# The first two attention tiles of a fused attention and two-layer MoE kernel: their heads in the hand-made order, a later start of the weight conversion, and two unread products per head

## Chip, cores and metric

The kernel runs on one core of one Trainium2 chip. The metric is the device time of one execution in microseconds. The kernel before takes 914.15 us (median of 3 runs, 914.04 to 915.16).

## What is computed

The reference is windowed causal attention over 4 batches, 8 heads, 576 positions and 64 columns a head (window 128, linear position bias), followed by a dense layer pair on all 2304 tokens and a mixture of 8 experts that sends each token to one expert. Cut to what matters:

```python
scores = where((rel >= 0) & (rel < 128), q @ k.T / 8 - slope[h] * abs(rel), -1e9)
x = softmax(scores) @ v                      # 2304 tokens x 512
x = (s * relu(x @ w_in)**2 + b) @ w_out      # 512 -> 2048 -> 512, dense
e = argmax(normalised(x) @ normalised(emb).T / tau)
out = gate * (relu(x @ w1[e]) @ w2[e])       # one of 8 experts per token
```

## The kernel before

**Tiles and heads.** The 2304 tokens are 18 tiles of 128. A tile has 8 heads, so there are 144 pairs of tile and head (called heads here, u = 8 t + h). Tiles 0 and 9 look at one tile of keys, the others at two. The first four tiles (`t < NRAW`) use the float32 inputs as they arrive (`raw`).

**One tick.** `tick` issues, in this order on TensorE (PE): the scores of head n (`stage_A`, L242), the value product of head n-4 (`stage_D`, L301), the transposes of head n-2 (`stage_C`, L278) and, once in four heads, the transposes of four finished heads (`stage_T`, L330). Around them stand, in the order of the string `'BX.C.M.G.N...'`: on VectorE (DVE) the bias and row minimum of head n (`stage_B`, L254) and the scaling of finished heads (`stage_X`); on ScalarE (ACT) the copy of the transposed head n-2 out of PSUM (`stage_C2`, L283, tile `PW`) and the exponential of head n (`stage_N`, L262). Each of the seven dots is a call of `pt`, which adds `rate[0]` to an account and takes one step of the conversion queue whenever the account reaches 1. The score banks are `bank[0:4]` in turn, so every fourth head uses `bank[3]`.

**The conversion.** The dense weights `w_in` and `w_out` come as 32 chunks of 512 KB into four `stage` buffers. A chunk is split in four steps of the queue: a load that refills a free buffer, a cast on ACT (L181), a merge on DVE (L185), and a last step with one instruction on ACT (L193) and one on DVE (L194). ACT and DVE work through their instructions in the order in which they were issued.

**The unread products.** `warm(n)` issues n products 128x128 by 128x512 of zeros in bfloat16 into `bank[3]` (L747); nothing reads them. Nine stand at the very start.

**The stretch of the change.** `ticks(2)` is 21: the 16 heads of tiles 0 and 1 and the first five of tile 2. The first 4 ticks stand inside `tc.manual_schedule()`, which leaves the order as written; the next 17 are ordered by the planner, by its own costs. Behind them a loop over `SK` = 8 weight chunks (called the first dense loop here) interleaves two heads with the first dense block's products `L1` (L351) and `L2` (L374); `first` and `second` force conversion steps where a chunk isn't there yet. That loop stays with the planner.

Of the kernel before, what the change touches and what calls it, by code (L numbers as in the profile page):

```python
# [43 lines left out]
def moe_attention_kernel(ctx, tc, qT, kT, vN, w_in, w_out, sc_s, sc_b, bneg, tri, bmix,  # L44
# [190 lines left out]
    def stage_A(u, S):  # L235
        t, h, order, sl, bc, n = geom(u)
        pr, odd = divmod(h, 2)
        hb = slice(64, 128) if odd else slice(0, 64)
        o = S[:, 0:n]
        if t < NRAW:  # L240
            for i, k in enumerate(order):
                nc.tensor.matmul(S[:, i * P:(i + 1) * P], lhsT=raws[1][t][hb, pr, :], rhs=raws[0][k][hb, pr, :], start=True, stop=True)  # L242
            return
        Q, K, L = (sp.QO, sp.KO, sp.LO) if odd else (sp.QE, sp.KE, sp.LE)
        nc.tensor.matmul(o, lhsT=Q[:, pr, :], rhs=K[:, pr, sl, :], start=True, stop=False)
        nc.tensor.matmul(o, lhsT=Q[:, pr, :], rhs=L[:, pr, sl, :], start=False, stop=True)

    def stage_B(u, S):
        t, h, order, sl, bc, n = geom(u)
        s, st = sbuf(u)[:, 0:n], st_r[u % 4]  # L250
        bi, c = (bias8[h], -0.125) if t < NRAW else (bias, 2.0 ** -(h + 1))
        if t in MIXED or t in AFTER_MIXED:
            bi, bc = bmx[t in AFTER_MIXED], slice(0, 256)
        nc.vector.tensor_tensor_reduce(s, S[:, 0:n], bi[:, bc], scale=c, scalar=3.0e38,  # L254
                                       op0=ALU.add, op1=ALU.min, accum_out=st[:, 0:1])
# [18 lines left out]
    def stage_C(u, PO):  # L274
        t, h, order, sl, bc, n = geom(u)
        p = sbuf(u) if t < NRAW else sp.p[u % 2]
        for i in range(len(order) if t < NRAW else 1):
            nc.tensor.transpose(PO[:, i * 128:(i + 1) * 128], p[:, i * 128:(i + 1) * 128], ident)  # L278

    def stage_C2(u, PO):  # L280
        t, h, order, sl, bc, n = geom(u)
        if t < NRAW:
            nc.scalar.activation(PW[u % 2][:, 0:n], PO[:, 0:n], AF.Copy)  # L283
            return
        pc, pp = (PP[u % 2][:, i] for i in range(2))
        nc.scalar.activation(pp if n > P else pc, PO[:, 0:P], AF.Copy)
        if n > P:
            nc.gpsimd.tensor_tensor(pc, pp, sp.tri, op=ALU.mult)
            nc.gpsimd.tensor_tensor(pp, pp, pc, op=ALU.subtract)
# [4 lines left out]
    def stage_D(u, PO):  # L294
        t, h, order, sl, bc, n = geom(u)
        last = len(order) - 1
        if t < NRAW:
            o = outs(u)[:, h % 4 * 64:(h % 4 + 1) * 64]
            for i, k in enumerate(order):
                v = raws[2][k].rearrange("p c f -> p (c f)")[:, h * 64:(h + 1) * 64]  # L300
                nc.tensor.matmul(o, lhsT=PW[u % 2][:, i * P:(i + 1) * P], rhs=v, start=i == 0, stop=i == last)  # L301
            return
        for i, k in enumerate(order):
            nc.tensor.matmul(PO[:, 0:P], lhsT=sp.V[k % 3][:, h // 2, :], rhs=PP[u % 2][:, t - k], start=i == 0, stop=i == last)

    def stage_X(u, PO, part=2):
        t, h = divmod(u, H)
        if t < NRAW:
            if h % 4 == 3 and part != 0:
                g = u // 4 % 2  # L310
                rs, xs = rs_r[g], xs_r[g]
                nc.vector.tensor_scalar(rs, su_r[t % 2][:, h - 3:h + 1], 1e-9, None, op0=ALU.add)
                nc.vector.reciprocal(rs, rs)
                nc.vector.tensor_tensor(xs.rearrange("p (h d) -> p h d", h=4), outs(u).rearrange("p (h d) -> p h d", h=4),
                                        rs.unsqueeze(2).to_broadcast([P, 4, 64]), op=ALU.mult)
            return
        pr, odd = divmod(h, 2)
        hb = slice(64, 128) if odd else slice(0, 64)
        blk, c = divmod(t, 2)
        xh, xl = (x[hb, pr, c * P:(c + 1) * P] for x in xbuf(blk))  # L320
        o = PO[hb, 0:P]
        if part != 1:
            nc.scalar.activation(xh, o, AF.Copy)
        if part != 0:
            nc.vector.tensor_tensor(xl, o, f32(xh), op=ALU.subtract)

    def stage_T(u):
        g = u // 4 % 2
        for i in range(2):
            nc.tensor.transpose(bank[4 + g][:, 256 + i * P:256 + (i + 1) * P], xs_r[g][:, i * P:(i + 1) * P], ident)  # L330
# [77 lines left out]
    def run(ops):  # L408
        for f in ops:
            if callable(f):  # L410
                f()
# [173 lines left out]
    rate, due = [0.0], [0.0]  # L585
# [9 lines left out]
    def plan_preps(t, h):  # L595

        if t < NRAW:
            return
        if h in (0, 1):
            preps.ops += prep_q(t, 2 + h)  # L600
            if h == 1 and t + 1 < NT:
                preps.ops.append(lambda: load_qkv(t + 1, 1))
        if t + 1 < NT:
            if h == HK:
                preps.ops += prep_k(t + 1)
                if t + 2 < NT:
                    preps.ops.append(lambda: load_qkv(t + 2, 0))
            if h == HV:
                preps.ops.append(lambda: load_qkv(t + 1, 2))
            if h in (5, 6):  # L610
                preps.ops += prep_q(t + 1, h - 5)
# [11 lines left out]
    def unit(n):  # L623

        n -= LAG if n >= NRAW * H + LAG else 0
        return n if 0 <= n < UN else None

    def ticks(t):

        return t * H + LAG + (LAG - 1 if t > NRAW else 0)  # L630

    OR0, OR, OR1 = 'BX.C.M.G.N...', '.BUC..VME.G[..R]', 'BUC.VE...MG[].R.'
    def tick(Sb, POb, mid=None, attend=True, Ob=None):
        n = nu[0] if attend else 2 * UN
        if attend:
            nu[0] += 1
        u, c, d, x = (None if NRAW * H <= i < NRAW * H + LAG else unit(i) for i in (n, n - 2, n - LAG + 1, n - LAG))
        if u is not None:
            S = Sb[u % len(Sb)]
            plan_preps(*divmod(u, H))  # L640
            stage_A(u, S)
        if d is not None:
            POd = Ob[d % len(Ob)] if Ob else POb[d % len(POb)][:, 256:512]
            stage_D(d, POd)
        if c is not None:
            POc = POb[c % len(POb)]
            stage_C(c, POc)
        turn = x is not None and x % 4 == 3 and x < NRAW * H
        if turn:
            stage_T(x)  # L650
        def B():
            if u is not None:
                stage_B(u, S)

        def X():
            if d is not None:
                stage_X(d, POd)

        def U():
            if d is not None:  # L660
                stage_X(d, POd, 0)

        def V():
            if d is not None:
                stage_X(d, POd, 1)

        def C():
            if c is not None:
                stage_C2(c, POc)

        def N():
            if u is not None:
                stage_N(u)
            if turn:
                stage_Y(x)

        def E():
            if u is not None:
                stage_N(u, 0)
            if turn:  # L680
                stage_Y(x)

        def R():
            if u is not None:
                stage_N(u, 1)

        def M():
            if mid is not None:
                mid(0)

        def G():
            if mid is not None:
                mid(fill if '[' in od else ())
            elif '[' in od:
                run(fill)

        fs = dict(E=E, R=R, U=U, V=V, B=B, X=X, C=C, N=N, M=M, G=G)
        od = OR0 if n < NRAW * H else (OR if mid is not None else OR1)
        fill = [pt if z == '.' else fs[z] for z in od[od.find('[') + 1:od.find(']')]] if '[' in od else []
        od = od[:od.find('[') + 1] + od[od.find(']') + 1:]  # L700
        for z in od:
            if z == '[':
                continue
            if z == '.':
                pt()
            else:
                fs[z]()
# [8 lines left out]
    wide = (bank[0:4], bank[4:8])  # L716
# [9 lines left out]
    HK, HV = 2, 5  # L726
    SK = 8
    J3 = 4
    LEAD = 4

    def need(c):
        while len(done) <= c:
# [11 lines left out]
    def warm(n):  # L744

        for _ in range(n):
            nc.tensor.matmul(bank[3], lhsT=zero[:, 0:P], rhs=zero, start=True, stop=True)  # L747

    warm(9)
    with tc.manual_schedule():  # L750
        for i in range(LEAD):
            tick(*wide)
            warm(1)
            if i == 1:
                rate[0] = 0.17
    for i in range(LEAD, ticks(2)):
        tick(*wide)
        warm(1)
    rate[0] = 0.4
    for j in range(SK):  # L760
        def mid(i):
# [339 lines left out]
```

## Time and profile before

| | |
|---|---|
| median of 3 runs | 914.15 us |
| the profiled execution | 915.15 us |
| its span | 913.4 us |
| PE busy | 896.0 us (98%) |
| ACT busy | 647.0 us (71%) |
| DVE busy | 642.2 us (70%) |
| mean granted clock of PE | 0.959 of 2.4 GHz |

The profile is of one execution. Busy times of PE are modelled from pipelined products: an engine that is busy all the time can still run at half its clock, so the granted clock is read beside them. The span leaves out some 1.75 us of the execution's own time.

### The profile page before, as it was taken

The page shows a single profiled execution, that of the slowest core. Times are in us where ns is not written, and L with a number is a line of the kernel's source. Part 1 is how long each engine was busy: PE and PEld are TensorE (multiplying, and loading weights), DVE is VectorE, ACT ScalarE, POOL GpSimd, SP SyncE. Part 2 cuts the span into 40 slices and gives each one's busy share as a digit, 9 for nine tenths or more (in the row PEclk, how much of TensorE's full clock was granted, in tenths as well). Part 3 has the DMA queues.
Part 4 walks back from the last instruction along what each step waited for, and adds up shares of the span by engine and source line. Part 5 has one row for each costly group of instructions (what it writes and reads, how often), then busy time and mean ns, then how long its engine had stood idle before and what let it go on. Part 6 is the DMA issues. An engine that isn't in the chain of part 4 may idle for free. (4 is left out here: it accounts for less than half of the span.)

```text
span 913.4 us, 17128 instructions
## 1 busy us (share of the span) xinstructions
PE 896.0 (98%) x5341; PEld 777.2 (85%) x5344; DVE 642.2 (70%) x1719; ACT 647.0 (71%) x1501; POOL 325.4 (36%) x553
## 2 busy tenths in 40 slices
PE   7999998999999999999999999999999999999997
PEld 4678877989999999999999999988888888888886
DVE  3336789656665676667666655467989999899895
ACT  4447897656676767666776753457889889888885
POOL 2000246554663266555655642111632111111101
PEclk7558999999999999999999999999999999999999
DMA  7224652010020102011200200456973795755300
GB/s 263 74 70 134 227 161 78 13 59 13 25 59 13 59 24 59 21 31 44 58 16 33 36 1 1 168 184 227 268 262 127 267 338 212 257 187 210 110 20 29
DMA packets 31600, 101.32 MB, mean 111 GB/s; under 512 B 8581, under 2 KB 9222, under 8 KB 24850
## 3 DMA queue, kind: packets, MB, share of 16 engines
q1 hardware_dynamic: 26562, 89.58, 29.4%
q0 software_dynamic: 4256, 9.46, 2.9%
q10 hardware_dynamic: 688, 1.15, 0.3%
q8 instruction: 43, 0.70, 0.3%
q14 instruction: 51, 0.42, 0.2%
HBM read 133.82 MB, written 10.92 MB: 158 GB/s over the span
## 5 line engine op out<-in xcount | busy, mean ns | idle before, releaser
L351 PE MATMUL bank<-XH,WIH 128*128 128x256 f32 x576 | 173.3, 301 | 0.8 <-ACT r L361 0.8
L351 PE MATMUL bank<-XH,WIL 128*128 128x256 f32 x576 | 163.7, 284 | 0.0
L351 PE MATMUL bank<-XL,WIH 128*128 128x256 f32 x576 | 163.4, 284 | 0.0
L363 DVE SCALAR_TENSOR_TENSOR bank<-bank,s_sb,r 128x256 f32<-128x256 f32 x112 | 55.1, 492 | 108.6 <-ACT r L361 108.2
L374 PE MATMUL bank<-WOH,GH 128*128 128x512 f32 x288 | 118.9, 413 | 0.5 <-ACT GH L364 0.5
L374 PE MATMUL bank<-WOH,GL 128*128 128x512 f32 x288 | 115.5, 402 | 1.1 <-DVE GL L366 1.1
L374 PE MATMUL bank<-WOL,GH 128*128 128x512 f32 x288 | 114.7, 398 | 0.0
L351 PEld LDWEIGHTS bank<-XH,WIH 128*128 128x128 f32 x576 | 110.6, 192 | 3.0 <-ACT r L361 1.0
L351 PEld LDWEIGHTS bank<-XL,WIH 128*128 128x128 f32 x576 | 110.4, 192 | 1.9 <-issue 0.2
L351 PEld LDWEIGHTS bank<-XH,WIL 128*128 128x128 f32 x576 | 109.9, 191 | 0.0
L364 ACT ACTIVATE GH<-bank,b_sb 128x256 fp32r<-128x256 f32 x112 | 53.2, 475 | 69.5 <-DVE bank L363 69.5
L262 ACT ACTIVATE s<-s,st 128x256 f32<-128x256 f32 (+1 forms) x144 | 71.2, 494 | 20.9 <-DVE st L254 17.7
L361 ACT ACTIVATE r<-bank 128x256 f32<-128x256 f32 x144 | 54.0, 375 | 44.5 <-PE bank L351 42.5
L830 PE MATMUL bank<-WIH,XH 128*128 128x512 f32 x192 | 77.7, 405 | 0.0
L254 DVE CUSTOM_DVE_ANT_0 s<-bank,bias 128x256 f32<-128x256 f32 (+1 forms) x112 | 44.7, 400 | 46.3 <-PE bank L242 32.5
L832 PE MATMUL bank<-WIL,XH 128*128 128x512 f32 x192 | 75.8, 395 | 0.0
L831 PE MATMUL bank<-WIH,XL 128*128 128x512 f32 x192 | 75.7, 394 | 0.0
L975 POOL DMA_INDIRECT out<-x,ids x23 | 28.1, 1223 | 133.4 <-ACT XH L959 109.3
L272 POOL TENSOR_SCALAR p<-p,st 128x128 f32<-128x128 f32 x104 | 42.5, 408 | 85.7 <-DVE st L265 69.7
L830 PE MATMUL bank<-WOH,XH 128*128 128x512 f32 x176 | 71.2, 405 | 0.0
L832 PE MATMUL bank<-WOL,XH 128*128 128x512 f32 x176 | 69.5, 395 | 0.0
L831 PE MATMUL bank<-WOH,XL 128*128 128x512 f32 x176 | 69.4, 394 | 0.0
(190 smaller groups left out, 2361.6 us busy)
## 6 DMA issues: line engine op xcount, KB each, us to landing
W1R<-w SPq DMA_DIRECT2D x46, 1024.0 KB
W2R<-w SPq DMA_DIRECT2D x46, 1024.0 KB
stage<-w_in SPq DMA_DIRECT2D x16, 512.0 KB
stage<-w_out SPq DMA_DIRECT2D x16, 512.0 KB
raw<-kT SPq DMA_DIRECT2D x18, 256.0 KB
raw<-qT SPq DMA_DIRECT2D x18, 256.0 KB
x1d<-stage SPq DMA_DIRECT2D x7, 512.0 KB
V<-vN SPq DMA_DIRECT2D x10, 256.0 KB
```

Of the source, the lines that this page charges most:

```text
L254: nc.vector.tensor_tensor_reduce(s, S[:, 0:n], bi[:, bc], scale=c, scalar=3.0e38, op0=ALU.add, op1=ALU.min, accum_out=st[:, 0:1])
L262: nc.scalar.activation(s, s, AF.Exp, bias=st[:, 0:1], scale=-1.0, accum_out=su)
L272: nc.gpsimd.tensor_scalar(p, p if n > P else s, st[:, 3:4], 1.0, op0=ALU.mult, op1=ALU.mult)
L351: nc.tensor.matmul(o, lhsT=w[j][:, c * P:(c + 1) * P], rhs=x[:, c, :], start=n == 0, stop=n == 11)
L361: nc.scalar.activation(r, o, AF.Relu)
L363: nc.vector.scalar_tensor_tensor(q, x, s_sb, r, op0=ALU.mult, op1=ALU.mult)
L364: nc.scalar.activation(gh, q, AF.Identity, bias=b_sb)
L374: nc.tensor.matmul(acc[k], lhsT=a[:, ts], rhs=w[j], start=(j == 0 and i == 0), stop=(j == NF - 1 and i == 2))
L830: nc.tensor.matmul(o, lhsT=lh, rhs=hi, start=first, stop=False)
L831: nc.tensor.matmul(o, lhsT=ll, rhs=hi, start=False, stop=False)
L832: nc.tensor.matmul(o, lhsT=lh, rhs=lo, start=False, stop=last)
L975: nc.gpsimd.indirect_dma_start(out=out[:, :], out_offset=bass.IndirectOffsetOnAxis(ids[:, 0:1], 0), in_=y, in_offset=None, bounds_check=NT ...
```

## The change

All 21 ticks stand inside the manual schedule. Conversion starts at the seventh tick instead of the third, with 0.25 steps a dot instead of 0.17. Each tick is followed by two unread products instead of one.

```diff
-    LEAD = 4
+    CONV = 6
+    LEAD = ticks(2)
...
     with tc.manual_schedule():
         for i in range(LEAD):
+            if i == CONV:
+                rate[0] = 0.25
             tick(*wide)
-            warm(1)
-            if i == 1:
-                rate[0] = 0.17
-    for i in range(LEAD, ticks(2)):
-        tick(*wide)
-        warm(1)
+            warm(2)
     rate[0] = 0.4
```

## Rows read from the trace of the kernel before

**Rows 1.** The page, part 2: granted PE clock in 40 slices, in tenths.
```profile
PEclk7558999999999999999999999999999999999999
```

**Rows 2.** Busy time by stretch of 5 us: length, PE, PEld, DVE, ACT, POOL, clock, DMA.
```profile
50.00:55.00 5.00, 4.64 (x18) 3.34 (x17) 0.71 (x4) 2.36 (x7) 0.00 (x0) 0.50 0.31 105
75.00:80.00 5.00, 5.00 (x25) 3.56 (x23) 2.17 (x7) 2.69 (x8) 0.00 (x0) 0.76 0.32 105
```

**Rows 3.** Waits in the first 75 us: us in total, times, longest.
```profile
DVE s L254 <- PE bank L242: 32.1, 20, 3.2
```

**Rows 4.** PE in order of time, first 40 us: start, us, operation, idle before it.
```profile
1.19 4.02 PE L747 MATMUL bank<-zero 128*128 128x512 bf16 x9 [1.19 <-DVE zero L530]
5.14 0.74 PE L242 MATMUL bank<-raw,raw 64*128 64x128 f32 x2
...
7.67 0.38 PE L747 MATMUL bank<-zero 128*128 128x512 bf16 x1
7.98 0.48 PE L242 MATMUL bank<-raw,raw 64*128 64x128 f32 x2
8.39 0.33 PE L278 MATMUL bank<-ident,s 128*128 128x128 f32 x1
12.35 0.56 PE L301 MATMUL bank<-raw,PW 128*128 128x64 f32 x2 [3.63 <-ACT PW L283]
```

**Rows 5.** ACT in order of time, first 40 us.
```profile
11.40 0.77 ACT L181 ACTIVATE tmp<-stage 128x512 f16<-128x512 bf16 x1 [3.81 <-DMA stage<-w_out]
12.04 0.25 ACT L283 ACTIVATE PW<-bank 128x128 f32<-128x128 f32 x1
...
12.57 0.77 ACT L181 ACTIVATE tmp<-stage 128x512 f16<-128x512 bf16 x1
```

**Rows 6.** Busy time by half microsecond where the clock changes.
```profile
12.50:13.00 0.50, 0.50 (x3) 0.43 (x4) 0.50 (x2) 0.50 (x3) 0.00 (x0) 0.52 1.01 164
...
152.50:153.00 0.50, 0.50 (x3) 0.43 (x2) 0.00 (x0) 0.48 (x2) 0.50 (x3) 0.50 0.00 0
...
599.50:600.00 0.50, 0.50 (x3) 0.37 (x2) 0.50 (x2) 0.00 (x0) 0.00 (x0) 0.61 0.98 410
```

**Rows 7.** PE in order of time, 40 to 84 us.
```profile
47.54 1.22 PE L242 MATMUL bank<-raw,raw 64*128 64x128 f32 x4
...
50.59 1.22 PE L242 MATMUL bank<-raw,raw 64*128 64x128 f32 x4
...
61.53 1.22 PE L242 MATMUL bank<-raw,raw 64*128 64x128 f32 x4
...
62.81 0.56 PE L351 MATMUL bank<-XH,WIH 128*128 128x256 f32 x1
...
79.04 0.71 PE L242 MATMUL bank<-raw,raw 64*128 64x128 f32 x4
...
80.32 0.37 PE L351 MATMUL bank<-XH,WIH 128*128 128x256 f32 x1
...
82.06 0.39 PE L374 MATMUL bank<-WOH,GH 128*128 128x512 f32 x1
82.30 0.39 PE L374 MATMUL bank<-WOL,GH 128*128 128x512 f32 x1
```

**Rows 8.** PE in order of time, ahead of the two later falls of the clock.
```profile
151.91 0.46 PE L304 MATMUL bank<-PP,raw 128*128 128x128 f32 x2 [1.92 <-POOL PP L289]
...
597.09 1.95 PE L441 MATMUL bank<-enT,tmp 128*128 128x8 f32 x16 [0.68 <-ACT tmp L452]
```

**Rows 9.** Groups of instructions by line, 12.5 to 61.5 us: busy, mean ns, idle before.
```profile
L254 DVE CUSTOM_DVE_ANT_0 s<-bank,bias 128x256 f32<-128x256 f32 (+1 forms) x18 | 6.9, 387 | 26.8 <-PE bank L242 26.8
...
L181 ACT ACTIVATE tmp<-stage 128x512 f16<-128x512 bf16 x7 | 5.4, 769 | 0.0
L185 DVE SCALAR_TENSOR_TENSOR stage<-stage,tmp 128x512 uint32<-128x512 uint32 x7 | 4.8, 682 | 4.5 <-ACT tmp L181 4.4
...
L193 ACT ACTIVATE WIH<-stage 128x512 fp32r<-128x512 f32 x3 | 2.0, 656 | 0.0
```

## The prediction, made before the result was known

> **What bounds the kernel now.** I began with the granted clock in the page's 40 slices [rows 1]: it is 0.7, 0.5, 0.5 and 0.8 in the first four (some 91 us) and 0.9 or more everywhere else. So the start is the one place where the kernel loses to the clock, and it is where the diff lies. The busy times by stretch [rows 2] show what bounds it there: from 50 to 55 us PE is busy for 4.64 of 5 us at clock 0.50 (1.2 GHz), while ACT is busy for 2.36. In the waits, DVE stood for 32.1 us of the first 75 because the scores weren't there yet [rows 3]. PE is the bound and it runs at half speed, though it is hardly ever idle.
>
> The timeline of PE shows how it came to that [rows 4]. Nine unread products run from 1.19 to 5.21 (0.45 us each, half clock). After them the products are short: the one at 7.67 takes 0.38, and the next instruction starts 0.31 behind it, which is the full clock. At 8.39 PE issues a transpose and then has nothing until 12.35: it waits 3.63 us for the copy `PW` on ACT. ACT, in turn, stood in front of a conversion cast that waited 3.81 us for its DMA and started at 11.40; the copy was issued behind it, at 12.04 [rows 5]. At 12.5 the clock falls to 0.50 [rows 6], and it comes back only at about 77.4 (the mean of 75 to 80 is 0.76 [rows 2]). So one wait of 3.63 us is followed by 65 us at half clock, in which heads alone, with one unread product each, don't bring it back; the long rows of dense products after 62.81 do.
>
> **The change, part by part.**
>
> The later start takes the cast out of the way of the first heads. With seven ticks at PE's own pace (below) the first cast reaches ACT at about 12 to 13 us. Its data were there at 11.40, and the second cast ran at 12.57 without a wait [rows 5], so I cost its wait at nothing; a DMA up to 2 us late would be covered too, since a head's exponential is wanted only two ticks after it. Then the gap of 3.63 us goes and nothing in the rows sends the clock down at 12.5. What is late next would be the score bank: every fourth head's scores are in `bank[3]`, where the unread products land, so in the written order these wait for DVE's reading of that bank. DVE's reading takes 0.39 us [rows 9] and PE has the value product and the transposes in between; I take 1 us in all for such waits, with bounds 0 and 7.
>
> The upper bound comes from ACT and DVE. A head's copy, exponential and read-out took ACT from 12.04 to 12.57 [rows 5], 0.53 us at 128 columns, at most 1.06 at 256. The conversion takes 7 x 0.25 = 1.75 steps a tick, 0.44 chunks, each with a cast of 0.77 and a second ACT instruction of 0.66 [rows 9]: 0.63 us. ACT needs 1.2 to 1.7 us a head. DVE needs 0.39 for the scores, 0.44 x 2 x 0.68 = 0.60 for the conversion [rows 9] and less than 0.4 for the rest, 1.4 us. Where a chunk's last step falls between two heads, the chain score, exponential, ACT part, DVE part is 0.39 + 0.3 + 0.66 + 0.68, about 2.0 to 2.3 us with the hand-overs, against the 1.83 that PE takes (below); were it so for 13 heads, that would be 6 us.
>
> A head of tiles 1 and 2 takes PE, at full clock, from 79.04 to 80.32 [rows 7]: 1.28 us for scores, values and transposes. Two unread products cost 0.24 (the pace of products of that size at 82.06 and 82.30 [rows 7]) plus 0.31 [rows 4], 0.55. So 1.83 a head. A head of tile 0 has one tile of keys: the scores take 0.41 (7.98 to 8.39 [rows 4]), values and transposes half of theirs, together 0.78, with the products 1.33. The lead from the first scores at 5.14 to the scores of head 21 is then 8 x 1.33 + 13 x 1.83 = 34.4; four turns of finished heads add 4 x 0.14 = 0.6, the values and transposes of the last heads fall behind it (-2.3), the first half microsecond still runs at half clock (+0.4), the bank waits add 1: 34.1, so head 21 starts at 39.2 instead of 61.53 [rows 7]. That is 22.3 us.
>
> Of those, the unread products by themselves cost 21 x 0.24 = 5.0 us at full clock by the row; at half clock 21 x 0.45 = 9.5. The Trainium skill, "TensorE: Matmul & The Clock Gate", section "Wait — 56ns, not 53.3ns?", gives 215.7 ns for such a product at the full clock, by which the same term would be an estimated 4.5 us; no sum here uses it.
>
> Behind the lead, the first two turns of the first dense loop ran at half clock, from 62.81 to 80.32 [rows 7], 17.5 us. At the price of a product of 512 columns at full clock against half (0.24 to 0.45) they'd take 9.3; as the later turns are not only products but hang on ACT too, I take 11.5 and gain 6.0, with bounds 3 and 8.
>
> The conversion is 19 x 1.19 = 22.6 steps in the lead before and 15 x 1.75 = 26.3 after: 3.7 steps, some 2.6 us of ACT and DVE together, earlier. It is hidden under PE; the first dense loop finds its chunks no later than before, so `need` forces no more than it did. Without that cover (ACT slower than PE) it is inside the 7 us. The loads are the same and SP's queue keeps its order; POOL gets nothing. The written order itself costs what the bank waits cost.
>
> Sum: 22.3 + 6.0 = 28.3 off the profiled execution's 915.15, which makes 886.9. That execution is 1.0 above the median of the runs, so I say 886.
>
> **The rivals.**
>
> *The clock holds through the lead* (chance 0.68): 886, within 880 (the dense loop's 8, no bank waits) and 895 (7 us of waits, the dense loop's 3). For it: from 5.8 to 8.7, with one unread product a head, the clock stood at full until PE was idle; the new lead has two and no such idle time.
>
> *It falls somewhere in the lead* (0.17), as at 152.5, behind 1.92 us of idle PE, and at 599.6, where only 0.68 us were idle but the products before had 8 columns [rows 6, 8]. The place would be a bank or conversion wait, or tiles that arrive late. Half-clock heads cost 3.05 (47.54 to 50.59 [rows 7]) + 0.45 = 3.5. A fall after head 13, at about 24 us, leaves 8 x 3.5 = 28: head 21 at 52, 9.5 us before its old time and no more gain, 905. By the place, 893 to 912.
> The rule in the Trainium skill, "TensorE: Matmul & The Clock Gate", section "Why this matters for your kernels", is that idle gaps between bursts send the clock back; by it alone the new lead keeps the clock, and 886 would be near certain. The fall at 599.6 behind small products with little idle time doesn't agree with that alone, which is why this rival keeps 0.17.
>
> *It never gets up, or falls before the seventh head* (0.15): the extra products decide, on the other side. With the clock at half from the start, 8 heads of tile 0 at 2.7 (twice 1.33) and 13 at 3.5, less 4.6 for the last heads' values, put head 21 at 67.6, 6.1 us later than before. With a fall at 9.5 us (four heads through, at 1.1 each since the first lack values) it's 9.5 + 4 x 2.7 + 45.5 - 4.6 = 61.2, 0.3 earlier. So 914 to 920. Against it: nine dense products stand ahead as before and brought the clock up. It decides from a fall before 12.5 us; later falls gain.
>
> **The numbers.** Predicted 886, the likeliest's. The range 879 to 912 takes in most of the first two cases (about 0.8); the first's own is 880 to 895. About 0.2% (2 us) is what a measurement of this kernel can tell from no change. Faster: 0.68 + 0.16 + 0.02 = 0.86; within: 0.04; slower: 0.10.
>
> **What would show it.** In the new profile: a clock of 1.0 from about 6 us on; no L283 wait behind L181 before 12 us; scores of head 21 at 38 to 41 us; heads of tile 1 at 1.8 to 2.0 us; ACT close to but under PE's pace; the dense loop's first turns under 6 us each. A clock of 0.5 anywhere from 6 to 50 us makes the prediction wrong, by 1.7 us a head behind it; so would the planner, if it orders the dense loop worse from its new start, or ACT above 1.9 us a head.

## The result, and the profile after

The changed kernel takes 886.5 us (median of 4 runs, 886.11 to 887.42) against 914.1 us of the kernel before on the same chip: a ratio of 0.9699, 95% interval 0.9683 to 0.9716. The forecast was 886. The profiled span went from 913.4 to 884.3 us, 29.1 us less.

The page of the changed kernel answers first: span, busy time of the engines, and the granted clock in 40 slices.

```profile
span 884.3 us, 17154 instructions
...
PE 872.0 (99%) x5365; PEld 757.1 (86%) x5365; DVE 641.5 (73%) x1719; ACT 647.1 (73%) x1501; POOL 321.6 (36%) x553
...
PEclk9999999999999999999999999999999999999999
```

The four slices below 0.9 of [rows 1] are gone. The trace has 24 PE instructions more (the change adds 21; it lacks a few of the unread products of the kernel before), and PE is busy for 24 us less; the other engines' busy times hardly moved. The stretches of 5 us that answer to [rows 2] (columns as there):

```profile
20.00:25.00 5.00, 4.97 (x32) 3.26 (x32) 2.92 (x11) 3.81 (x12) 0.00 (x0) 1.00 0.43 121
30.00:35.00 5.00, 5.00 (x33) 3.42 (x31) 3.42 (x9) 4.20 (x13) 0.00 (x0) 1.00 0.46 161
```

PE is still the bound, but at full clock, and does 32 products in 5 us where it did 18. ACT has come close: 4.20 of 5. DVE's wait for the scores was 32.1 us in the first 75 us of the kernel before [rows 3]; in the first 48 us of the changed kernel, which hold about the same work, it is 13.4. PE waited once for DVE to read `bank[3]`:

```profile
DVE s L254 <- PE bank L242: 13.4, 12, 5.0
...
PE bank L748 <- DVE st L254: 0.3, 1, 0.3
```

PE in order of time, changed kernel, the rows that answer to [rows 4, 7]:

```profile
5.14 0.79 PE L242 MATMUL bank<-raw,raw 64*128 64x128 f32 x2
5.87 0.85 PE L748 MATMUL bank<-zero 128*128 128x512 bf16 x2
6.66 0.48 PE L242 MATMUL bank<-raw,raw 64*128 64x128 f32 x2
...
9.73 0.59 PE L748 MATMUL bank<-zero 128*128 128x512 bf16 x2 [0.27 <-DVE st L254]
...
26.58 0.71 PE L242 MATMUL bank<-raw,raw 64*128 64x128 f32 x4
...
28.46 0.71 PE L242 MATMUL bank<-raw,raw 64*128 64x128 f32 x4
...
37.49 0.36 PE L351 MATMUL bank<-XH,WIH 128*128 128x256 f32 x1
...
41.31 0.71 PE L242 MATMUL bank<-raw,raw 64*128 64x128 f32 x4
...
53.89 0.28 PE L351 MATMUL bank<-XH,WIH 128*128 128x256 f32 x1
...
55.41 0.71 PE L242 MATMUL bank<-raw,raw 64*128 64x128 f32 x4
```

From the second pair of scores (6.66) on, everything runs at full clock. A head of tile 1 takes 1.88 us (26.58 to 28.46). The scores of head 21 start at 41.31 instead of 61.53, and the planner has by then put six dense products (from 37.49) ahead of them. The third turn of the first dense loop starts at 53.89 instead of 80.32. These two landmarks don't mark the same work in both kernels. By head 21 the changed kernel has done six dense products that the kernel before does later, and by the third turn four (it has then done all six products of an `L2`, the kernel before two). At the scores of head 26 the work done is the same in both, the second unread products apart. They start at 55.41, and in the kernel before at 82.86:

```profile
82.86 0.71 PE L242 MATMUL bank<-raw,raw 64*128 64x128 f32 x4
```

On ACT nothing stands in front of head 0's copy any more, which runs at 8.39 instead of 12.04 [rows 5]; the first cast comes at 14.14:

```profile
8.39 0.28 ACT L283 ACTIVATE PW<-bank 128x128 f32<-128x128 f32 x1 [0.27 <-PE bank L278]
...
14.14 0.77 ACT L181 ACTIVATE tmp<-stage 128x512 f16<-128x512 bf16 x1
```

A landmark further on is DVE's only copy of the router's matrix (instructions that write `enT`), in the kernel before and in the changed one; the last figures are its start:

```profile
L396 DVE COPY enT<-bank x1: 192/192/192, 199.4 to 199.4; 128x32 f32<-128x32 f32 x1
```

```profile
L396 DVE COPY enT<-bank x1: 192/192/192, 170.1 to 170.1; 128x32 f32<-128x32 f32 x1
```

The changed kernel is thus 20.2 us ahead at head 21, 26.4 at the third turn of the dense loop, 27.4 at head 26, 29.3 at the router's setup and 29.1 at the end.

### The profile page after: what moved, and what is told of

Its sections match the earlier page's. It is cut to its first block, busy times and chain, and to the rows that moved or that the text cites. A ratio compares the mean times of both kernels' runs of the same rounds, so it can differ in the third digit from the quotient of the medians.

```text
span 884.3 us, 17154 instructions
## 1 busy us (share of the span) xinstructions
PE 872.0 (99%) x5365; PEld 757.1 (86%) x5365; DVE 641.5 (73%) x1719; ACT 647.1 (73%) x1501; POOL 321.6 (36%) x553
## 5 line engine op out<-in xcount | busy, mean ns | idle before, releaser
L351 PEld LDWEIGHTS bank<-XH,WIH 128*128 128x128 f32 x576 | 108.6, 189 | 4.3 <-ACT r L361 2.1
L374 PEld LDWEIGHTS bank<-WOH,GL 128*128 128x128 f32 x288 | 54.4, 189 | 15.8 <-DVE GL L366 4.0
```

The lines of the kernel that those rows point to most:

```text
L351: nc.tensor.matmul(o, lhsT=w[j][:, c * P:(c + 1) * P], rhs=x[:, c, :], start=n == 0, stop=n == 11)
L374: nc.tensor.matmul(acc[k], lhsT=a[:, ts], rhs=w[j], start=(j == 0 and i == 0), stop=(j == NF - 1 and i == 2))
```

## The experiments

Two of the theories were there from the prediction. **A**: PE's idle time behind the early cast sends the clock down, and it's enough to take that wait away. **B**: the second product a head keeps the clock up. The rival **C** came with them: the planner's order puts waits into the lead. **D** was formed after the first four runs: two products a head bring a low clock up again, one doesn't. Each kernel was compared with the kernel before on the same chip.

**One product a head.** The changed kernel with

```diff
-            warm(2)
+            warm(1)
```

> The changed kernel with one unread product a head instead of two; hand-made order and late conversion kept. Theory A (the wait of PE behind the cast is what sent the clock down; without it the clock holds with one product too): 21 products of 0.21 us less, so 882 us, clock 1.0 through the lead. Theory B (the second product keeps the clock up): the clock falls in the lead, heads of tile 1 at 3.05 us from there, 900 to 912 us.

Measured: three of its five executions took 882.3 to 884.9 us (0.9678, 0.9634 to 0.9721), the other two 899.7 and 911.0. The profile is of the longest. PE in order of time, and one stretch of 5 us:

```profile
5.86 0.61 PE L748 MATMUL bank<-zero 128*128 128x512 bf16 x1
...
8.66 0.63 PE L748 MATMUL bank<-zero 128*128 128x512 bf16 x1
```

```profile
5.00:10.00 5.00, 5.00 (x14) 2.48 (x14) 0.90 (x6) 1.64 (x7) 3.13 (x7) 1.00 1.04 408
```

An unread product of the kernel before takes the same time in the stretch from 50 to 55 us, where the clock is 0.50 [rows 2]; at full clock it takes 0.38 [rows 4]:

```profile
50.02 0.63 PE L747 MATMUL bank<-zero 128*128 128x512 bf16 x1
```

So this execution runs at half clock from the first head on: the nine products hadn't brought the clock up, although the granted clock is given as 1.00. A's 882 was met in three executions, in which the time says that the clock was up. The profiled one isn't B's case either, as its clock didn't fall but never rose; the one of 899.7 us has no trace.

**The conversion as early as before.** Hand-made order and two products, with `rate[0] = 0.17` from the third head.

```diff
-            if i == CONV:
-                rate[0] = 0.25
+            if i == 2:
+                rate[0] = 0.17
```

> The changed kernel with the conversion as before (from the third head, 0.17 steps a dot); hand-made order and two products kept. Theory A: the copy stands behind the cast until about 11.4 us again, PE is idle for 2 to 3 us, the clock falls at about 12 us, heads of tile 1 at 3.5 us: 912 to 920 us. Theory B: the two products keep the clock up all the same: 886 to 890 us.

Measured: 884.2 us, 0.968 (0.9649 to 0.9712), as fast as the changed kernel. A's 912 to 920 is missed by far, and B's 886 to 890 by 2 us. ACT in order of time:

```profile
8.07 0.76 ACT L181 ACTIVATE tmp<-stage 128x512 f16<-128x512 bf16 x1
8.69 0.25 ACT L283 ACTIVATE PW<-bank 128x128 f32<-128x128 f32 x1
```

The first cast runs at 8.07 and waits for nothing. So the early start wasn't what made ACT wait. The order of ACT's instructions tells what was: in the kernel before, the planner had put the cast of the second chunk (`stage1`, from `w_out`) ahead of the first chunk's and ahead of head 0's copy. The row of [rows 5] says so: it names the DMA `stage<-w_out`.

**The planner's order.** Late conversion and two products; only the first four ticks inside the manual schedule.

```diff
     with tc.manual_schedule():
-        for i in range(LEAD):
+        for i in range(4):
...
+    for i in range(4, LEAD):
+        head(i)
```

> The changed kernel with only the first four ticks in the hand-made order, the other 17 left to the planner as before; late conversion and two products kept. Theory A: the order is worth little at full clock, 884 to 890 us, clock 1.0. Rival C: the planner's order puts a wait into PE's lead and the clock falls: 895 us or more.

Measured: 891.5 us, 0.9766 (0.9734 to 0.9797). ACT, then PE in order of time, then stretches of 1 us:

```profile
7.97 0.77 ACT L181 ACTIVATE tmp<-stage 128x512 f16<-128x512 bf16 x1 [5.30 <-DMA stage<-w_in]
9.51 0.66 ACT L193 ACTIVATE WIH<-stage 128x512 fp32r<-128x512 f32 x1 [0.76 <-DVE stage L185]
11.19 0.40 ACT L262 ACTIVATE s<-s,st 128x128 f32<-128x128 f32 x1 [1.03 <-DVE st L254]
```

```profile
11.15 0.86 PE L242 MATMUL bank<-raw,raw 64*128 64x128 f32 x4 [3.80 <-DVE st L254]
...
15.59 1.89 PE L748 MATMUL bank<-zero 128*128 128x512 bf16 x4
...
18.80 0.59 PE L748 MATMUL bank<-zero 128*128 128x512 bf16 x2
```

```profile
12.00:13.00 1.00, 1.00 (x4) 0.30 (x3) 0.00 (x0) 0.62 (x4) 0.00 (x0) 0.50 0.70 84
...
18.00:19.00 1.00, 1.00 (x7) 0.59 (x5) 0.30 (x2) 0.95 (x2) 0.00 (x0) 0.81 1.15 311
```

The planner carries the cast and the last step of chunk 0, written behind the seventh head, to the very front of ACT, before the first exponential. The first four ticks being written by hand didn't keep it from that. PE is idle for 3.80 us, the clock falls at about 12 and is back at about 18, behind four unread products in a row that the planner had bunched. That return gave rise to D. C's mechanism holds, a wait of PE in the lead and a fall of the clock. Its size of 895 us or more doesn't: the kernel is only some 5 us slower than the changed one, with the clock back after 6 us. Part of the 5 us lies elsewhere, as the clock falls once more between 125 and 135 us (0.76 and 0.90 in its two stretches of 5 us).

**The late conversion alone.** As the run before, with `warm(1)`: the kernel before with only the conversion's start and rate changed.

> The kernel before with nothing changed but the conversion's start and rate (seventh head, 0.25 steps a dot); planner's order from the fifth head, one product a head. Theory A: this alone does it, 880 to 887 us, clock 1.0 in the lead. Theories B and C: the clock falls in the lead, 900 us or more.

Measured: 906.9 us, 0.9932 (0.9905 to 0.9959). PE in order of time:

```profile
10.14 0.79 PE L242 MATMUL bank<-raw,raw 64*128 64x128 f32 x2 [3.07 <-DVE st L254]
...
15.62 0.63 PE L748 MATMUL bank<-zero 128*128 128x512 bf16 x1
```

The same cast at the front, PE idle for 3.07 us, and half clock to about 60 us. The late start alone doesn't take the wait away, since the planner undoes it.

**Without the nine products at the start.** The line `warm(9)` left out, two products a head.

> The changed kernel without the nine unread products at the very start; two products a head kept. Theory D (two products a head bring the clock up in the lead by themselves, one does not): half clock in the first heads, full within some 7 us of them, 887 to 893 us. Theory A (only idle time moves the clock; nothing in the heads brings it up): half clock to the dense products, 905 to 915 us.

Measured: 911.9 us, 0.9999 (0.9963 to 1.0035). D falls. PE in order of time:

```profile
4.60 0.76 PE L242 MATMUL bank<-raw,raw 64*128 64x128 f32 x2 [4.60 <-DMA raw<-qT]
...
6.99 1.04 PE L748 MATMUL bank<-zero 128*128 128x512 bf16 x2
...
62.95 1.08 PE L748 MATMUL bank<-zero 128*128 128x512 bf16 x2
...
65.83 0.59 PE L748 MATMUL bank<-zero 128*128 128x512 bf16 x2
```

Two products take 1.04 us, against 0.59 to 0.60 at full clock, and it stays so up to the pair at 62.95, ahead of head 20: two at a time among the short products don't bring the clock up. It is up at 65.83, behind six dense products (61.52 to 62.95) and that pair.

**The same with one product a head.**

> The changed kernel without the nine products at the start and with one product a head. Theory D: the clock never comes up in the lead, products of 0.63 us until the dense ones, 905 to 912 us. Theory A gives the same; if the clock comes up, D falls: 882 to 890 us.

Measured: 909.7 us, 0.9943 (0.9908 to 0.9979). PE in order of time:

```profile
8.16 0.63 PE L748 MATMUL bank<-zero 128*128 128x512 bf16 x1
```

Half clock again, and no difference in kind. The 2.2 us between the two runs are within their intervals.

**The order alone.** The kernel before with all 21 ticks inside the manual schedule, conversion and one product as before.

> The kernel before with all 21 ticks in the hand-made order and nothing else changed: conversion from the third head, one product a head. Theory D: the planner's order made the gap and its end here brings the gain when the nine products have the clock up, 880 to 884 us, and some 910 us in an execution where they haven't. Theory B (the second product is needed to hold the clock): it falls, 900 us or more in every execution.

Measured: single executions of 881.7, 897.7, 902.3 and 904.0 us, too far apart for an interval. The profile, of the longest, PE in order of time:

```profile
10.23 0.38 PE L748 MATMUL bank<-zero 128*128 128x512 bf16 x1
...
12.00 0.43 PE L301 MATMUL bank<-raw,PW 128*128 128x64 f32 x2 [0.98 <-ACT PW L283]
...
14.46 0.59 PE L748 MATMUL bank<-zero 128*128 128x512 bf16 x1 [0.80 <-DVE st L254]
...
17.25 0.63 PE L748 MATMUL bank<-zero 128*128 128x512 bf16 x1
```

The clock was up behind the nine products (0.38 us at 10.23), two waits of 0.98 and 0.80 us followed, and it fell. The order alone can bring the whole gain (881.7), but not in every execution. Neither expectation is met: B has no room for 881.7, and D none for a fall behind nine products that had brought the clock up.

**One cast moved back.** The changed kernel with the cast of the second chunk ahead of head 0's copy, where the planner had it:

```diff
+            if i == 2:
+                conv.ops.remove(ops[1][1])
+                ops[1][1]()
             tick(*wide)
```

> The changed kernel with one instruction moved: the cast of the second weight chunk stands on ACT ahead of head 0's copy, where the planner of the kernel before put it. PE has to wait for it until about 10 us, less what it has to do. Theory D: PE idle for 1 to 3 us, the clock falls at 10 to 13 us and two products a head bring it back within some 7 us: 888 to 895 us. Theory A: it falls and stays down: 910 us or more.

Measured: 917.2 us, 1.0042 (1.0021 to 1.0063). ACT and PE in order of time, and a later stretch of 5 us:

```profile
10.30 0.77 ACT L181 ACTIVATE tmp<-stage 128x512 f16<-128x512 bf16 x1 [2.75 <-DMA stage<-w_out]
```

```profile
11.25 0.43 PE L301 MATMUL bank<-raw,PW 128*128 128x64 f32 x2 [1.08 <-ACT PW L283]
...
11.79 0.93 PE L748 MATMUL bank<-zero 128*128 128x512 bf16 x2
12.65 0.79 PE L242 MATMUL bank<-raw,raw 64*128 64x128 f32 x2
```

```profile
15.00:20.00 5.00, 5.00 (x16) 2.69 (x15) 1.70 (x8) 1.94 (x7) 0.00 (x0) 0.50 0.83 300
```

One instruction in the wrong place takes the whole gain, and 3 us more. PE was idle for 1.08 us only, as it had two products a head to do in the meantime; the clock fell all the same and stayed down. That is A's case and not D's.

**The same with one product a head.**

> As the run before it (the second chunk's cast ahead of head 0's copy) with one product a head. Theory D: the clock falls behind PE's wait and stays at half until the dense products, 907 to 915 us, close to the kernel before though the order is by hand. If order or late conversion were what counts and not the wait: 882 to 890 us.

Measured: 909.0 us, 0.9965 (0.9948 to 0.9982). PE in order of time:

```profile
12.11 0.59 PE L301 MATMUL bank<-raw,PW 128*128 128x64 f32 x2 [2.69 <-ACT PW L283]
...
12.76 0.63 PE L748 MATMUL bank<-zero 128*128 128x512 bf16 x1
```

The kernel with one product and no cast moved took 882.3 to 884.9 us where its clock was up. With the same order and the same late conversion the wait and what follows from it thus cost 24 to 27 us. The second product costs some 8 us here (917.2 against 909.0).

**Two products for eight heads, then one.** With the early conversion of the second experiment:

```diff
-            warm(2)
+            warm(2 if i < 8 else 1)
```

> Hand-made order, conversion from the third head at 0.17 steps a dot, two products for the first eight heads and one for the other thirteen. Theory D (one holds the clock once it is up): 13 products of 0.21 us less than with two throughout, 881 us. Theory B: the clock falls behind the eighth head, 895 to 905 us.

Measured: 881.4 us, 0.9656 (0.963 to 0.9682), all executions between 880.3 and 882.6. PE in order of time:

```profile
15.79 0.38 PE L748 MATMUL bank<-zero 128*128 128x512 bf16 x1 [0.59 <-DVE st L254]
```

This kernel and the one with the order alone differ in nothing but the second product of the first eight heads (they ran on different chips). There PE waited for 0.98 and 0.80 us and the clock fell; here the first of these waits is gone, the second is 0.59, and all five executions are fast.

**Two products for eight heads, then none** (`warm(2 if i < 8 else 0)`).

> As the run before it, with no product from the ninth head on. If the attention products alone hold the clock: 13 x 0.55 us less than with two throughout, 877 to 880 us. If they don't: the clock falls at 15 to 20 us, heads at about 2.6 us, 893 to 903 us.

Measured: 879.1 us, 0.9642 (0.9611 to 0.9674). PE in order of time, and a stretch of 5 us:

```profile
15.90 0.38 PE L748 MATMUL bank<-zero 128*128 128x512 bf16 x1 [0.58 <-DVE st L254]
...
18.89 0.71 PE L242 MATMUL bank<-raw,raw 64*128 64x128 f32 x4
```

```profile
30.00:35.00 5.00, 5.00 (x38) 4.13 (x37) 4.38 (x14) 4.98 (x16) 0.00 (x0) 1.00 0.33 105
```

The attention heads hold the full clock by themselves once they are past the start, in all four executions by their times (878.9 to 881.4). ACT is now busy for 4.98 of 5 us, so there's little more to have in this stretch. This is the fastest version found, and it beats both kernels.

**The changed kernel again**, beside the last three.

> The changed kernel itself, for comparison on the same chip: 885 to 888 us.

Measured: 886.2 us, 0.9708 (0.9681 to 0.9734).

## Why the prediction was right, and where it wasn't

**The clock is the gain: right.** Undoing it with one instruction gave 917.2 us, with everything else in place. The third rival had that case at 914 to 920. Its other case, a clock that never gets up, was nearer to 912: 911.9 without the nine products.

**The wait behind a cast sends it down: right. That the later start removes it: wrong.** "The later start takes the cast out of the way of the first heads" is the step that failed. With the early start and the hand-made order the time is 884.2; with the late start and the planner's order it's 891.5 with two products and 906.9 with one. The cast that waited was the second chunk's, and it stood there because the planner had moved it. It's the hand-made order that takes the wait away, and the prediction had costed that order at nothing but its bank waits. As the change brings both, the wait went all the same, and the sum came out although this step was wrong.

**The lead: 22.3 us forecast, 20.2 measured at head 21.** 0.8 of the difference are the six dense products that the planner put ahead of it (37.49 to 38.28); at equal work the lead gave 21.0. For the same reason the scores of head 21 at 41.31 lie just behind the sign of 38 to 41. The rest is the head of 1.88 instead of 1.83 us, 0.7 over 13 heads, and smaller things. The waits for `bank[3]`, taken at 1 us, show as one of 0.27 and a few shorter delays.

**The dense loop: 6.0 forecast, 6.4 measured** at equal work: 27.4 at head 26 less 21.0. The 6.2 between the two landmarks above (26.4 less 20.2) is close to it by chance, since the six products ahead of the first and the four ahead of the second nearly cancel.

**Not in the sum: 1.7 us behind head 26** (29.1 less 27.4). The fall of the clock at 152.5 [rows 6, 8] has no counterpart: no stretch of the changed kernel between 100 and 565 us is below 1.00. By the router's setup the gain is 1.9 (29.3 less 27.4), and 0.2 are lost again; how the 1.9 divide between that fall and the planner's new order was not tried.

**The sum: 886 forecast, 886.5 measured, and in part luck.** The lead gave 1.3 us less than its term at equal work, the dense loop 0.4 more, and 1.7 us came from a stretch of which the prediction said nothing.

**The two unread products: the price right, the use only in part.** At full clock a pair takes 0.59 us and a single one 0.38, so the second costs 0.21, where the forecast had 0.24. For 13 of them that makes 2.7 of the 4.8 us between two kernels (886.2 less 881.4). The rest may be the early conversion's, in which they differ too: its own run took 884.2 us, 2.0 less than 886.2, but on another chip and not clear of noise. Once PE has to wait behind the cast they don't hold the clock (917.2), and two a head don't bring it up among the short products (911.9). What speaks for them are the first eight heads. With two there and the hand-made order untouched, all 22 executions of four kernels (the changed one twice) took 878.9 to 887.4 us, and the five traces show full clock through the lead. With one, 4 of 9 executions of two kernels were as fast. The traces show two ways to lose with one: the clock never rose (one product a head, 911.0), or it rose and fell behind two waits (the order alone, 904.0). They also show where two can help. In the changed kernel the clock rose only during the first pair of unread products (0.85 us at 5.87, against 0.60 for a pair at full clock and 1.04 at half), and the second products fill a part of PE's waits (0.98 and 0.80 against none and 0.59). So it is shown that two in the first eight heads matter; why some executions with one keep the clock is open. Whether two always bring it up is open too: one execution with the cast moved back, which has the same first heads, took 917.2 us with a mean granted clock of 1.00, as executions do whose clock never rose, and it has no trace.

## What to carry to other kernels

Where a stretch is slow at a busy PE, read the duration of a known product before anything else; then look for the instruction that stood ahead of the one PE waited for, and by whose hand it came there. An order written by hand for a few ticks wasn't kept here, because the planner ordered what follows and moved later instructions ahead of it. Unread products were worth their price only where the clock was in danger, here in the first eight heads, not wherever it was low. And two kernels are to be compared at points that have the same work behind them: an order that changes moves the landmarks too.

## What the runs showed of the hardware that wasn't expected

An idle time of PE of 1.08 us, in a stretch with two wide products a head, was followed by the half clock (one cast moved back), one of 0.58 us wasn't (two products, then none). The length of the wait isn't all: in the kernel before, 0.68 us among products of 8 columns came ahead of a fall [rows 6, 8]. The Trainium skill, "TensorE: Matmul & The Clock Gate", section "Why this matters for your kernels", names longer gaps as the ones to avoid. The traces don't agree: shorter ones were followed by a fall here.

The same short products hold a clock that is up and don't bring up one that is down. From the ninth head on they ran at full clock with no unread product at all (two products, then none; 1.00 from 30 to 35 us). In the kernel before, with one unread product a head, they ran at half clock for 49 us (12.5 to 61.5), with PE busy for at least 4.64 us in each stretch of 5 us from 15 us on.

The granted clock in the profile is not always to be trusted: it stood at 1.00 in the run with one product whose products took 0.61 to 0.63 us, the half clock's duration. The mean over an execution misleads in the same way: two executions of the kernel before, measured beside that run, took 913.2 and 913.3 us with means of 0.959 and 0.962, and a third took 913.2 with 0.996. The durations decide.
